# Moving a pool of SBUF tiles and a few queued steps in a chunk-attention and FFN kernel

## The chip, the cores and the metric

The kernel runs on one core of one Trainium2 chip. The metric is the device time of one execution in microseconds (us). The profile is of one such execution; its trace holds every instruction of the five engines: TensorE (PE, with its weight loads shown apart as PEld), VectorE (DVE), ScalarE (ACT), GpSimd (POOL) and SyncE (SP, which only issues DMAs here).

## The reference

Attention inside chunks of 64 positions, then a normalised two-layer FFN with a residual. B = 8, H = 8, S = 576, D = 64, so 4608 rows of 512; the hidden layer has 2048 columns. All data is fp32.

```python
scores = matmul(q_c, k_c^T) / sqrt(D)          # per (batch, head, chunk of 64)
attn = exp(scores - max); attn = attn / (sum(attn) + 1e-9)
x = matmul(attn, v_c)                           # regrouped to (B, S, H * D)
xn = (x - mean(x)) / sqrt(var(x) + 1e-6) * g_ln
out = x + maximum(xn @ w_ch1, 0) @ w_ch2        # 512 -> 2048 -> 512
```

## The kernel before, in words

**Rows.** The 4608 rows are 18 pairs of 256 rows; two pairs are a tile, so there are nine tiles of 512 rows. Tiles 0 to 2 go through the FFN one by one (`ffn`); tiles 3 to 8 go in three units of two tiles (`unit_ffn`). Attention for a pair (`attention`) is a generator; so are the FFN streams. Nothing is scheduled by a tool: `play` reads strings of letters and takes one step of the named stream for each letter, and `weave` takes steps of side streams at given points of a unit. Each engine runs its own instructions in the order in which they were issued, so the strings and the places of the calls decide what stands behind what.

**Precision.** A product is done as three TensorE passes on split operands: a rounded high part (`h`) and the rest, the low part (`l`): high by high, high by low, low by high. A hidden block is made ready in two steps: a cast, ACT's Relu into the high part (L540 in `ffn`, L799 in a unit), and a rest, DVE's difference (L541 and L804).

**Tiles 1 and 2.** `SECOND` is the order of the side steps during tile 1's FFN, `THIRD` the one during tile 2's. The number is that of a token of the FFN (`u` is a block of 12 matmuls, up or down; `1` is the cast and rest behind an up block) before which the letters' steps are taken. `A` and `B` are the attention of tile 2's two pairs, `C` and `G` those of tile 3's, `D` and `H` those of tile 4's. `S` is `prepare`, which writes combined and split weights to DRAM for the units: for each of eight pairs of hidden blocks, sums on POOL (L635, then L643 to L646), a cast on ACT (L654), a rest on POOL (L656) and DMAs. `P` and `Q` are `combine`, which makes the units' operands from the transposed rows. In `attention`, the transposes of the probabilities are four steps of four DVE instructions (L358) or TensorE transposes, `den` is the step with the sums (L365 to L367), then come the 64 small output matmuls (L387), the step that scales them to `x` (L421), statistics, and transposes of the normalised rows (L467 on DVE, or L459 on TensorE with ACT's copy L460).

**Units.** The up product of a unit is done by a scheme with seven block products (2, 1, 6, 5, 7, 3, 4) in place of eight, for each of four quarters `q` of the hidden blocks and each of two halves `e`. Each block product is 6 matmuls (L777) into one of four PSUM banks; ACT copies a bank to SBUF (`snap`, L783) or DVE adds one to a snap (`hu`, L786). After the four quarters come two down halves, `n` = 0 and 1, each over 16 hidden blocks `f` with 12 matmuls of 512 columns (L860). Blocks get their cast and rest (`split`, `rest`) three blocks ahead. Block number i of a unit's 32 lies in the pool `hp` (tiles `hh`, `hl`) where i % 5 is 0 or 1, and in tiles `hx` of the pool `raws` where it is 2, 3 or 4; `raws` also holds the snaps of the up product. TensorE loads these blocks as the stationary operand and streams the weights (`ring`). Attention for the pairs of the next unit is woven into the first two units; the third has no side work.

**SBUF.** Pools lie one behind the other in the order in which they are made. Adding up their tiles per partition, `raws` (12 KiB) is the last and lies at 209.6 to 221.6 KiB; `x` (`keep`, four tiles of 4 KiB) lies at 152.3 to 168.3 KiB; `xt` (the ring and the transposed rows) and `hp` lie between them, `hp` ending at 208.3 KiB.

Of the kernel before, what the change touches and what calls it, by code (L numbers as in the profile page):

```python
# [10 lines left out]
F32R = mybir.dt.float32r  # L11
# [6 lines left out]
P = 128  # L18
B, H, S, D = 8, 8, 576, 64
DM = H * D  # L20
# [5 lines left out]
HP = H // 2  # L26
NK = DM // P
NF = DFF // P
# [8 lines left out]
UNITS = (NTILE - LEAD) // 2  # L37

SECOND = {
    0: "ABS", 1: "AS", 2: "S", 3: "AAS", 4: "AS", 5: "AAS", 6: "S", 7: "AS", 8: "AAS", 9: "AAS", 10: "AAS", 11: "BAS",  # L40
    12: "BAC", 13: "BS", 14: "S", 15: "BBS", 16: "BS", 17: "BBS", 18: "S", 19: "BS", 20: "BBCS", 21: "BBS", 22: "BBDS",
    23: "BCS", 24: "BC", 25: "CS", 26: "S", 27: "CCS", 28: "CS", 29: "CCS", 30: "CDS", 31: "CDDS", 32: "DS",
}
THIRD = {
    0: "CS", 1: "CS", 2: "DDG", 3: "D", 4: "DD", 5: "D", 6: "DG", 7: "GGH", 8: "DG", 9: "D", 10: "GGP", 11: "HGP",
    12: "GGP", 13: "GHP", 14: "GGHP", 15: "GHP", 16: "GP", 17: "HHGP", 18: "HGG", 19: "HGP", 20: "HP", 21: "HP",
    22: "H", 24: "H", 25: "H", 26: "QQ", 27: "QR", 28: "Q", 29: "QXXN", 30: "QQR", 31: "Q",
}
ROOMS = {1: (3, 9), 2: (6,)}

# [47 lines left out]
def chunk_attention_ffn(ctx: ExitStack, tc: tile.TileContext, qkv, v01, g, w, out):  # L98
# [3 lines left out]
    const = ctx.enter_context(tc.tile_pool(name="const", bufs=1))  # L102
    load = ctx.enter_context(tc.tile_pool(name="load", bufs=1))
    work = ctx.enter_context(tc.tile_pool(name="work", bufs=2))
    keep = ctx.enter_context(tc.tile_pool(name="keep", bufs=4))
    xtp = ctx.enter_context(tc.tile_pool(name="xt", bufs=2))
    hp_ = ctx.enter_context(tc.tile_pool(name="hp", bufs=2))
    small = ctx.enter_context(tc.tile_pool(name="small", bufs=4))
    gap = ctx.enter_context(tc.tile_pool(name="gap", bufs=1))
    gap.tile([P, 16], F32, name="gap")  # L110
    raws = ctx.enter_context(tc.tile_pool(name="raws", bufs=1))
    ps_a = ctx.enter_context(tc.tile_pool(name="ps_a", bufs=1, space=PSUM))
    ps_h = ctx.enter_context(tc.tile_pool(name="ps_h", bufs=2, space=PSUM))
    ps_y = ctx.enter_context(tc.tile_pool(name="ps_y", bufs=4, space=PSUM))
# [513 lines left out]
    def prepare():  # L628
        late = []
        for p in range(NF // 2):  # L630
            fe, q, e = 2 * p, p // 2, p % 2
            both = [wp[fe], wp[fe + 1]]
            t_ = raws.tile([P, 2, 2, PAIR], F32, name="sums", tag="wf")
            for i in range(2):
                nc.gpsimd.tensor_tensor(  # L635
                    out=t_[:, i], in0=both[i][:, 0, :DM].rearrange("p (a n) -> p a n", a=2).bitcast(F32),
                    in1=both[i][:, 1, :DM].rearrange("p (a n) -> p a n", a=2).bitcast(F32), op=ALU.add,
                )
            for i in range(2):
                nc.sync.dma_start(w2d[fe + i], both[i][:, :, DM:].bitcast(F32))  # L640
            yield
            a11, a12, a21, a22 = t_[:, 0, 0], t_[:, 0, 1], t_[:, 1, 0], t_[:, 1, 1]
            nc.gpsimd.tensor_tensor(out=a22, in0=a21, in1=a22, op=ALU.add)  # L643
            nc.gpsimd.tensor_tensor(out=a21, in0=a11, in1=a21, op=ALU.subtract)
            nc.gpsimd.tensor_tensor(out=a11, in0=a22, in1=a11, op=ALU.subtract)
            nc.gpsimd.tensor_tensor(out=a12, in0=a12, in1=a11, op=ALU.subtract)  # L646
            for to, of in late:
                nc.sync.dma_start(to, of.bitcast(F32))
            nc.sync.dma_start(wa[q][:, e, 0], both[0][:, :, PAIR:DM].bitcast(F32))
            nc.sync.dma_start(wa[q][:, e, 1], both[0][:, :, :PAIR].bitcast(F32))  # L650
            nc.sync.dma_start(wa[q][:, 6, e], both[1][:, :, PAIR:DM].bitcast(F32))
            yield
            r = raws.tile([P, 2, 2, 2, PAIR], F32R, name="parts", tag="raw")
            nc.scalar.copy(r[:, 0], t_)  # L654
            yield
            nc.gpsimd.tensor_tensor(out=r[:, 1], in0=t_, in1=r[:, 0].bitcast(F32), op=ALU.subtract)  # L656
            late = [
                (wa[q][:, 2 + e, 0], r[:, :, 0, 0]), (wa[q][:, 4 + e, 1], r[:, :, 0, 1]),
                (wa[q][:, 4 + e, 0], r[:, :, 1, 0]), (wa[q][:, 2 + e, 1], r[:, :, 1, 1]),
            ]  # L660
            yield
        for to, of in late:
            nc.sync.dma_start(to, of.bitcast(F32))
        yield
# [93 lines left out]
    def unit_ffn(u):  # L758
# [29 lines left out]
        more = []  # L788
# [19 lines left out]
        for q in range(NF // 4):  # L808
            banks = [ps_y.tile([P, DM], F32, name="y") for _ in range(4)]
            c_, a_ = banks[0::2], banks[1::2]  # L810
            h = [hu[2 * q], hu[2 * q + 1]]
            s = [snaps[:3], snaps[3:]]

            def pair_of():
                w = ring.take()[:, : 2 * DM].rearrange("p (i h n) -> p i h n", i=2, h=2)
                return w[:, 0], w[:, 1]

            steps = []
            for e in range(2):
                steps += [  # L820
                    (c_, e, "2", None),
                    (a_, e, "1", lambda e: (copy(s[e][0], a_[e]), add(h[e][:, 0, 0], c_[e], s[e][0]))),
                ]
            for e in range(2):
                steps += [
                    (a_, e, "6", lambda e: copy(s[e][1], a_[e])),
                    (c_, e, "5", lambda e: copy(s[e][2], c_[e])),
                ]
            for e in range(2):
                steps += [  # L830
                    (a_, e, "7", lambda e: add(h[e][:, 1, 1], a_[e], s[e][2])),
                    (c_, e, "3", lambda e: add(h[e][:, 1, 0], c_[e], s[e][1])),
                ]
            for e in range(2):
                steps += [(a_, e, "4", lambda e: copy(h[e][:, 0, 1], a_[e]))]
            for i, (bank, e, name, then) in enumerate(steps):
                if i % 2 == 0:
                    w01 = pair_of()
                product(bank[e], w01[i % 2], name, name in "215")
                yield 6  # L840
                if i % 2:
                    ring.fetch()
                if then:
                    then(e)
                if q == NF // 4 - 1 and name in "34":
                    (split if name == "3" else rest)(e)

        for n, g in ((2, "raw"), (1, "wf")):
            x = raws.tile([P, n, 2, DM], F32R, name="hx", tag=g)
            more.extend(x[:, i] for i in range(n))  # L850
        ahead = 3
        split(2)
        stores = []
        for n in range(2):
            ys = [ps_y.tile([P, DM], F32, name="y") for _ in range(4 - 2 * n)]
# [7 lines left out]
                )  # L863

            pairs = [first + 2 * n, first + 2 * n + 1]
            ws = {}
            for f in range(NF):
                ws[f] = ring.take()[:, : 2 * DM].rearrange("p (h n) -> p h n", h=2)
                if f < NF - 2:
                    i = n * NF + f + ahead  # L870
                    for at, (m, j) in enumerate(
                        [(m, j) for j in range(4) for m in range(3)] if f == 0 else
                        [(m, j) for m in range(3) for j in range(4)]
                    ):
                        down(f, ws[f], j, m)
                        if at % 4 == 3:
                            yield 4
                            if at == 3 and n == f == 0:
                                rest(2)
                            if at == 3 and f > 0 and i - 1 < 2 * NF:  # L880
                                split(i - 1)
                            if at == 7 and f > 0 and i - 1 < 2 * NF:
                                rest(i - 1)
                    ring.fetch()
                    if f == 6:
                        for pair in pairs:
                            back[pair] = unspill(pair)
                    for to, of in stores:
                        nc.sync.dma_start(to, of)
                    stores.clear()  # L890
            for j in range(4):
                for f in range(NF - 2, NF):
                    for m in range(3):
                        down(f, ws[f], j, m)
                yield 6
                pair, jj = pairs[j // 2], j % 2
                x = back[pair][:, jj, :]
                nc.vector.tensor_tensor(out=x, in0=ys[j], in1=x, op=ALU.add)
                row = pair * PAIR + jj * P
                if tail and n == 1:  # L900
                    nc.sync.dma_start(out[row : row + P, :], x)
                else:
                    stores.append((out[row : row + P, :], x))
                if n == 0 and j < 3:
                    split(NF + j)
                    rest(NF + j)
            ring.fetch()
            ring.fetch()
        for to, of in stores:
# [113 lines left out]
```

## Time and profile before

| what | value |
|---|---|
| time, median of 3 runs | 853.22 us (852.88 to 853.78) |
| the profiled execution's time | 852.65 us |
| its span in the trace | 850.9 us |
| PE busy, PEld busy | 836.7 us (98%), 682.4 us |
| DVE, ACT, POOL busy | 563.1, 271.1, 150.7 us |
| TensorE clock granted, mean | 0.999 |
| tile 1, tile 2 FFN (about) | 123 to 222 us, 222 to 329 us |
| units: up product, then down halves | 329 to 411 to 505; 505 to 588 to 682; 682 to 758 to 851 us |

Times inside the trace are counted from the start of the span. Each row of a group gives its count, busy time and mean duration in ns, then the idle time of its engine just before it and what ended it. In rows in order of time, the first number is the start, the second how long the merged instructions took; consecutive matmuls overlap in these rows, so the rate of matmuls is read from starts, not from durations.

### The profile page before, as it was taken

To read this page: it belongs to the slowest core of one execution; us is meant where nothing else is said; L and a number is where in the kernel's file an instruction comes from. 1 tells how busy PE (TensorE), PEld (TensorE's weight loads), DVE (VectorE), ACT (ScalarE), POOL (GpSimd) and SP (SyncE) were. 2 spreads that over 40 slices of the span, in tenths; PEclk is the share of its full clock that TensorE was granted. 3 is DMA by queue.
4 is the path that set the end of the run, shared out by engine and by line. 5 is a ranking of instruction groups with operands and counts; after the bars stand their busy time and mean duration, and the time that the engine had idled before them with its cause. 6 is when DMAs were issued, how large, how long until landed. Compare 5 with 4: busy or idle time off the path is not lost.

```text
span 850.9 us, 14618 instructions
## 1 busy us (share of the span) xinstructions
PE 836.7 (98%) x5850; PEld 682.4 (80%) x5850; DVE 563.1 (66%) x957; ACT 271.1 (32%) x425; POOL 150.7 (18%) x138
## 2 busy tenths in 40 slices
PE   7999999999999999999999999999999999999998
PEld 4888888878787888888787888887878888888886
DVE  6999957777546926797999927879999421232321
ACT  5766432222312322222342402334223222232220
POOL 0110006585701223000130400001302200000000
PEclk9999999999999999999999999999999999999999
DMA  9996508977860137776686768867658776656572
GB/s 361 331 301 184 192 7 288 328 273 257 315 199 26 62 138 260 232 251 201 247 313 211 290 182 292 280 211 248 235 200 269 238 244 195 189 194 241 191 274 104
DMA packets 69043, 192.60 MB, mean 226 GB/s; under 512 B 6640, under 2 KB 20976, under 8 KB 67056
## 3 DMA queue, kind: packets, MB, share of 16 engines
q1 hardware_dynamic: 67680, 186.95, 63.9%
q0 software_dynamic: 1296, 4.72, 2.9%
q8 instruction: 46, 0.75, 0.3%
q14 instruction: 21, 0.17, 0.1%
HBM read 147.08 MB, written 39.85 MB: 220 GB/s over the span
## 4 chain that ended last, share of the span: by engine, by line
PE 78%; DVE 15%; issue 2%; POOL 2%; ACT 1%; DMA 1%; SPq 0%; POOLq 0%; ACTq 0%; DVEq 0%
PE y L777 24%; PE y L860 14%; PE h L527 14%; PE y L551 13%; PE h L860 8%; DVE pt_sb L358 4%; DVE rows L467 3%; PE s L298 2%; DVE hx L804 1%; DVE hl L804 1%; DVE den L365 1%; DVE xt L500 1%; PE s L387 1%; DMA k_t<-qkv 1%; PE h L387 1%
## 5 line engine op out<-in xcount | busy, mean ns | idle before, releaser
L777 PE MATMUL y<-xc,ring 128*128 128x512 f32 x1008 | 232.0, 390 | 0.0
L777 PEld LDWEIGHTS y<-xc,ring 128*128 128x128 f32 x1008 | 188.4, 188 | 39.5
L860 PE MATMUL y<-ring,hx 128*128 128x512 f32 x486 | 130.7, 396 | 0.0
L527 PE MATMUL h<-xth,wp 128*128 128x512 f32 (+1 forms) x432 | 129.9, 371 | 0.6 <-DVE x L421 0.5
L860 PEld LDWEIGHTS y<-ring,hx 128*128 128x128 f32 x486 | 91.1, 188 | 21.1
L786 DVE TENSOR_TENSOR hu<-y,snap 128x512 f32<-128x512 f32 x72 | 49.2, 690 | 83.5 <-ACT snap L783 43.3
L551 PE MATMUL y<-wp,hh 128*128 128x512 f32 x376 | 96.3, 394 | 0.0
L527 PEld LDWEIGHTS h<-xth,wp 128*128 128x128 f32 x432 | 78.3, 188 | 15.8 <-DVE hl L541 1.0
L783 ACT COPY snap<-y 128x512 f32<-128x512 f32 x72 | 42.2, 587 | 121.8 <-PE y L777 121.8
L551 PEld LDWEIGHTS y<-wp,hh 128*128 128x128 f32 x376 | 69.1, 188 | 14.0
L730 POOL TENSOR_TENSOR xc<-rows,xc 128x512 fp32r<-128x512 f32 x42 | 58.1, 1397 | 125.5 <-ACT xc L729 120.8
L358 DVE STREAM_TRANSPOSE pt_sb<-p_sb 32x256 f32<-32x256 f32 x176 | 76.7, 436 | 3.5 <-ACT p_sb L333 0.5
L527 PE MATMUL h<-xtl,wp 128*128 128x512 f32 (+1 forms) x216 | 78.3, 367 | 0.0
L541 DVE SCALAR_TENSOR_TENSOR hl<-h,hh 128x512 fp32r<-128x512 f32 (+1 forms) x53 | 32.9, 627 | 66.4 <-ACT hh L540 66.0
L860 PE MATMUL y<-ring,hh 128*128 128x512 f32 x252 | 70.5, 390 | 0.0
L467 DVE STREAM_TRANSPOSE rows<-xg 32x256 f32<-32x256 f32 x144 | 62.7, 435 | 5.4 <-ACT xg L449 3.2
L804 DVE SCALAR_TENSOR_TENSOR hx<-hu,hx 128x512 fp32r<-128x512 f32 x54 | 42.8, 798 | 30.7 <-PE y L860 12.6
L540 ACT ACTIVATE hh<-h 128x512 fp32r<-128x512 f32 (+1 forms) x53 | 28.5, 545 | 104.7 <-PE h L527 104.7
L860 PEld LDWEIGHTS y<-ring,hh 128*128 128x128 f32 x252 | 47.4, 188 | 10.2
L437 POOL TENSOR_TENSOR rstd<-vare,mhalf 128x2 f32<-128x2 f32 x12 | 10.6, 885 | 241.1 <-DVE vare L436 241.1
L551 PE MATMUL y<-wp,hl 128*128 128x512 f32 x188 | 51.8, 390 | 0.0
L860 PE MATMUL h<-ring,hx 128*128 128x512 f32 x162 | 50.8, 394 | 0.0
(130 smaller groups left out, 992.9 us busy)
## 6 DMA issues: line engine op xcount, KB each, us to landing
ring<-w2d SPq DMA_DIRECT2D x96, 512.0 KB, 4.1
ring<-wa SPq DMA_DIRECT2D x84, 512.0 KB, 4.3
raw<-w SPq DMA_DIRECT2D x15, 1024.0 KB, 7.8
out<-x SPq DMA_DIRECT2D x36, 256.0 KB, 4.5
q_t<-qkv SPq DMA_DIRECT2D x17, 512.0 KB, 5.6
k_t<-qkv SPq DMA_DIRECT2D x17, 512.0 KB, 6.5
v_t<-qkv SPq DMA_DIRECT2D x32, 256.0 KB, 6.0
w2d<-wp SPq DMA_DIRECT2D x16, 512.0 KB, 6.0
```

The lines of the kernel that those rows point to most:

```text
L358: nc.vector.transpose(out=pt_sb[quad(2 * h2 + j), :, c, quad(i)], in_=p_sb[quad(2 * c + i), :, h2, quad(j)])
L467: nc.vector.transpose(out=to[quad(j), :, quad(i)], in_=of[quad(i), :, quad(j)])
L527: nc.tensor.matmul(h, lhsT=(wh, wh, wl)[m][:, ks], rhs=(xth, xtl, xth)[m][:, k, :], start=i == 0, stop=i == len(terms) - 1,)
L540: nc.scalar.activation(hh, h, AF.Relu)
L541: nc.vector.scalar_tensor_tensor(out=hl, in0=h, scalar=0.0, in1=hh.bitcast(F32), op0=ALU.max, op1=ALU.subtract)
L551: nc.tensor.matmul(sums(pairs[j // 2])[j % 2], lhsT=(hh, hh, hl)[m], rhs=(wh, wl, wh)[m], start=f == 0 and m == 0, stop=f == NF - 1 and m ...
L730: nc.gpsimd.tensor_tensor(out=o[:, 1], in0=x, in1=o[:, 0].bitcast(F32), op=ALU.subtract)
L777: nc.tensor.matmul(bank, lhsT=w[:, (0, 0, 1)[m], ks], rhs=x[:, (0, 1, 0)[m], k, :], start=start and k == m == 0, stop=k == 1 and m == 2, s ...
L783: nc.scalar.copy(out, bank)
L786: nc.vector.tensor_tensor(out=out, in0=bank, in1=s, op=ALU.add)
L804: nc.vector.scalar_tensor_tensor(out=hl, in0=x, scalar=0.0, in1=hh.bitcast(F32), op0=ALU.max, op1=ALU.subtract)
L860: nc.tensor.matmul(ys[j], lhsT=(hh, hh, hl)[m], rhs=w[:, (0, 1, 0)[m]], start=f == 0 and m == 0, stop=f == NF - 1 and m == 2,)
```

## The change

Three things are changed. The pool `keep` is made after `raws` instead of before `xt`: so `x` moves to the last 16 KiB that are used, 205.6 to 221.6 KiB, and `xt`, `hp`, `small` and `raws` each move down by 16 KiB (`raws` to 193.6 to 205.6 KiB). In the last quarter of a unit's up product, the casts and rests of blocks 0, 1 and 2 are issued with block products 7, 3 and 4 instead of 3, 4 and after them, and in a down half's first block the order of the matmuls is changed so that the four that need the low part come last; the rests at the turn from n = 0 to n = 1 are issued one bank later. In the strings, `prepare` gets one more (empty) step per pair of blocks between its sums and its cast, for which 8 letters `S` are added, two in `SECOND` and six in `THIRD`; and steps of the streams `A`, `B`, `G`, `H` and `P` are moved by one to three tokens.

```diff
-    0: "ABS", 1: "AS", 2: "S", 3: "AAS", 4: "AS", 5: "AAS", 6: "S", ...
-    12: "BAC", 13: "BS", 14: "S", 15: "BBS", 16: "BS", 17: "BBS", 18: "S", 19: "BS", ...
-    23: "BCS", 24: "BC", ...
+    0: "ABS", 1: "AS", 2: "S", 3: "AAS", 4: "AS", 5: "AS", 6: "AS", ...
+    12: "BACS", 13: "BS", 14: "S", 15: "BBS", 16: "BS", 17: "BS", 18: "BS", 19: "BS", ...
+    23: "BCS", 24: "BCS", ...
...
-    0: "CS", 1: "CS", 2: "DDG", 3: "D", 4: "DD", 5: "D", 6: "DG", 7: "GGH", 8: "DG", 9: "D", 10: "GGP", 11: "HGP",
-    12: "GGP", 13: "GHP", 14: "GGHP", 15: "GHP", 16: "GP", 17: "HHGP", 18: "HGG", 19: "HGP", 20: "HP", 21: "HP",
-    22: "H", 24: "H", ...
+    0: "CS", 1: "CS", 2: "DDGS", 3: "DS", 4: "DDS", 5: "DS", 6: "DGS", 7: "GGHS", 8: "DG", 9: "D", 10: "GGP",
+    11: "HGGP", 12: "G", 13: "G", 14: "GGHP", 15: "GHP", 16: "GHP", 17: "GP", 18: "HHGP", 19: "HGP", 20: "HGP",
+    21: "HHP", 22: "HP", 24: "H", ...
...
     work = ctx.enter_context(tc.tile_pool(name="work", bufs=2))
-    keep = ctx.enter_context(tc.tile_pool(name="keep", bufs=4))
     xtp = ctx.enter_context(tc.tile_pool(name="xt", bufs=2))
...
     raws = ctx.enter_context(tc.tile_pool(name="raws", bufs=1))
+    keep = ctx.enter_context(tc.tile_pool(name="keep", bufs=4))
...
             yield
+            yield
             r = raws.tile([P, 2, 2, 2, PAIR], F32R, name="parts", tag="raw")
             nc.scalar.copy(r[:, 0], t_)
...
-                if q == NF // 4 - 1 and name in "34":
-                    (split if name == "3" else rest)(e)
-
-        for n, g in ((2, "raw"), (1, "wf")):
-            x = raws.tile([P, n, 2, DM], F32R, name="hx", tag=g)
-            more.extend(x[:, i] for i in range(n))
+                if q == NF // 4 - 1 and name in "73":
+                    (split if name == "7" else rest)(e)
+                if q == NF // 4 - 1 and name == "4":
+                    if e == 0:
+                        for n, g in ((2, "raw"), (1, "wf")):
+                            x = raws.tile([P, n, 2, DM], F32R, name="hx", tag=g)
+                            more.extend(x[:, i] for i in range(n))
+                    (rest if e else split)(2)
+
         ahead = 3
-        split(2)
...
+            early, late = ((2, 3, 0), 1) if n else ((0, 2, 1), 3)
+            firsts = [(m, j) for m in range(2) for j in early] + [(0, late), (1, late)] + [(2, j) for j in (*early, late)]
...
-                        [(m, j) for j in range(4) for m in range(3)] if f == 0 else
+                        firsts if f == 0 else
...
-                            if at == 3 and n == f == 0:
-                                rest(2)
+                            if at == 3 and n > f == 0:
+                                rest(NF + 2)
...
                 if n == 0 and j < 3:
                     split(NF + j)
-                    rest(NF + j)
+                if n == 0 and 0 < j < 3:
+                    rest(NF + j - 1)
```

More of the change, by code (lines that the diff above doesn't have):

```diff
@@ L39 @@
 SECOND = {
-    0: "ABS", 1: "AS", 2: "S", 3: "AAS", 4: "AS", 5: "AAS", 6: "S", 7: "AS", 8: "AAS", 9: "AAS", 10: "AAS", 11: "BAS",
-    12: "BAC", 13: "BS", 14: "S", 15: "BBS", 16: "BS", 17: "BBS", 18: "S", 19: "BS", 20: "BBCS", 21: "BBS", 22: "BBDS",
-    23: "BCS", 24: "BC", 25: "CS", 26: "S", 27: "CCS", 28: "CS", 29: "CCS", 30: "CDS", 31: "CDDS", 32: "DS",
+    0: "ABS", 1: "AS", 2: "S", 3: "AAS", 4: "AS", 5: "AS", 6: "AS", 7: "AS", 8: "AAS", 9: "AAS", 10: "AAS", 11: "BAS",
+    12: "BACS", 13: "BS", 14: "S", 15: "BBS", 16: "BS", 17: "BS", 18: "BS", 19: "BS", 20: "BBCS", 21: "BBS", 22: "BBDS",
+    23: "BCS", 24: "BCS", 25: "CS", 26: "S", 27: "CCS", 28: "CS", 29: "CCS", 30: "CDS", 31: "CDDS", 32: "DS",
 }
 THIRD = {
-    0: "CS", 1: "CS", 2: "DDG", 3: "D", 4: "DD", 5: "D", 6: "DG", 7: "GGH", 8: "DG", 9: "D", 10: "GGP", 11: "HGP",
-    12: "GGP", 13: "GHP", 14: "GGHP", 15: "GHP", 16: "GP", 17: "HHGP", 18: "HGG", 19: "HGP", 20: "HP", 21: "HP",
-    22: "H", 24: "H", 25: "H", 26: "QQ", 27: "QR", 28: "Q", 29: "QXXN", 30: "QQR", 31: "Q",
+    0: "CS", 1: "CS", 2: "DDGS", 3: "DS", 4: "DDS", 5: "DS", 6: "DGS", 7: "GGHS", 8: "DG", 9: "D", 10: "GGP",
+    11: "HGGP", 12: "G", 13: "G", 14: "GGHP", 15: "GHP", 16: "GHP", 17: "GP", 18: "HHGP", 19: "HGP", 20: "HGP",
+    21: "HHP", 22: "HP", 24: "H", 25: "H", 26: "QQ", 27: "QR", 28: "Q", 29: "QXXN", 30: "QQR", 31: "Q",
 }
```

## The prediction

> **What bounds the kernel now.** I read the page first, then the waits, then PE's and DVE's rows in order of time.
>
> ```profile
> span 850.9 us, 14618 instructions
> PE 836.7 (98%) x5850; PEld 682.4 (80%) x5850; DVE 563.1 (66%) x957; ACT 271.1 (32%) x425; POOL 150.7 (18%) x138
> PE y L860 <- DVE hl L804: 2.3, 4, 0.9
> ```
>
> PE is busy for 98% of the span, so a change can gain in two ways only: by closing PE's stops, or by letting its matmuls follow each other faster. The wait row says that in the units PE stopped four times for a rest (L804), 0.9 us at the longest.
>
> Matmuls overlap, so their pace has to be read from starts. The third unit has no side work:
>
> ```profile
> 764.00 8.53 PE L860 MATMUL y<-ring,hx 128*128 128x512 f32 x36
> 772.37 1.98 PE L860 MATMUL y<-ring,hh 128*128 128x512 f32 x8
> 777.82 8.53 PE L860 MATMUL y<-ring,hx 128*128 128x512 f32 x36
> 786.19 1.98 PE L860 MATMUL y<-ring,hh 128*128 128x512 f32 x8
> 791.63 6.44 PE L860 MATMUL y<-ring,hx 128*128 128x512 f32 x27
> L860 PE MATMUL y<-ring,hx 128*128 128x512 f32 x486 | 130.7, 396 | 0.0
> L860 PE MATMUL y<-ring,hh 128*128 128x512 f32 x252 | 70.5, 390 | 0.0
> L860 PE MATMUL h<-ring,hx 128*128 128x512 f32 x162 | 50.8, 394 | 0.0
> L860 PE MATMUL h<-ring,hh 128*128 128x512 f32 x84 | 25.9, 389 | 0.0
> ```
>
> 36 matmuls that load `hx` take 772.37 - 764.00 = 8.37 us, 232.5 ns each, twice alike; the 24 on `hh` and `hl` from 786.19 to 791.63 take 226.7 ns each. The mean durations (396 and 394 against 390 and 389) say the same. Shape, clock and streamed ring are the same; what differs is where the stationary operand lies: `hx` above 209.6 KiB, `hh` and `hl` below 208.3 KiB. That is 5.8 ns on 486 + 162 = 648 matmuls, 3.8 us in all.
>
> Now the turn from block products to down halves, in the first unit (the second has the same rows 176.8 us later), where attention for the next unit is woven in:
>
> ```profile
> 411.55 0.61 PE L860 MATMUL y<-ring,hh 128*128 128x512 f32 x2
> 413.07 0.50 PE L860 MATMUL y<-ring,hl 128*128 128x512 f32 x1 [0.90 <-DVE hl L804]
> 456.05 0.62 PE L860 MATMUL y<-ring,hh 128*128 128x512 f32 x2
> 456.84 0.51 PE L860 MATMUL y<-ring,hl 128*128 128x512 f32 x1 [0.16 <-DVE hl L804]
> 411.50:456.00 44.50, 43.60 (x364) 34.93 (x364) 42.10 (x78) 16.14 (x28) 10.76 (x8) 1.00 0.71 249
> 430.34 1.35 DVE L804 SCALAR_TENSOR_TENSOR hx<-hu,hx 128x512 fp32r<-128x512 f32 x1 [1.13 <-ACT hx L799]
> 454.53 1.21 DVE L365 TENSOR_REDUCE den<-p_sb 128x16 f32<-128x1024 f32 x1
> 456.15 0.63 DVE L804 SCALAR_TENSOR_TENSOR hl<-hu,hh 128x512 fp32r<-128x512 f32 x1
> ```
>
> The third matmul of the half needs block 0's low part and waits until 413.07. The row of the stretch 411.5 to 456 (columns: PE, PEld, DVE, ACT, POOL) is the more important one: DVE is busy for 42.10 of 44.50 us, with one idle time over 0.2 us, the 1.13 shown. Block 15's rest (456.15) stands behind `den` and ends just as PE wants it. In the first down half of units 1 and 2 DVE is as much the bound as PE; in the second halves (34 of 49.5 us busy) and the third unit it isn't.
>
> **The change part by part.** *Stops in tiles 1 and 2.*
>
> ```profile
> 177.68 1.05 ACT L654 CAST parts<-sums 128x1024 fp32r<-128x1024 f32 x1 [4.39 <-POOL sums L646]
> 183.59 1.22 DVE L365 TENSOR_REDUCE den<-p_sb 128x16 f32<-128x1024 f32 x1
> 185.40 0.33 PE L387 MATMUL h<-v_t,pt_sb 64*64 64x64 f32 x4
> 186.38 1.15 PE L387 MATMUL h<-v_t,pt_sb 64*64 64x64 f32 x60 [0.65 <-DVE hl L541]
> 187.46 2.12 PE L551 MATMUL y<-wp,hh 128*128 128x512 f32 x8
> 230.40 1.05 ACT L654 CAST parts<-sums 128x1024 fp32r<-128x1024 f32 x1 [2.74 <-POOL sums L646]
> 231.99 0.66 PE L459 MATMUL s<-ident,xg 128*128 128x128 f32 x4 [0.79 <-ACT rows L460]
> 263.06 5.40 DVE L358 STREAM_TRANSPOSE pt_sb<-p_sb 32x256 f32<-32x256 f32 x12
> 271.13 0.34 PE L387 MATMUL h<-v_t,pt_sb 64*64 64x64 f32 x6
> 271.72 1.14 PE L387 MATMUL h<-v_t,pt_sb 64*64 64x64 f32 x58 [0.26 <-DVE pt_sb L358]
> 272.80 2.11 PE L551 MATMUL y<-wp,hh 128*128 128x512 f32 x8
> 274.74 1.07 PE L551 MATMUL y<-wp,hl 128*128 128x512 f32 x4
> 276.34 0.50 PE L527 MATMUL h<-xth,wp 128*128 128x512 f32 x1 [0.53 <-DVE x L421]
> ACT parts L654 <- POOL sums L646: 14.7, 5, 4.4
> ```
>
> The idle times in brackets are 0.65 + 0.79 + 0.26 + 0.53 = 2.23 us; each stop also costs a restart. By starts: 64 output matmuls take 1.09 us where nothing holds them (58 of them run from 271.72 to 272.80), but last from 185.40 to 187.46, 0.97 lost; the stop before 231.99 is 0.79 and a restart of some 0.16, 0.95 lost; 271.13 to 272.80 loses 0.58; four matmuls from 274.74 last 1.60 in place of 0.91, 0.69 lost. Sum 3.2 us.
>
> The first: `B`'s `den` (steps of 1.22, 0.65 and 0.25 us) stands on DVE ahead of the rest that frees the PSUM bank; token 18 puts it behind. DVE was late there because ACT's L654 waited 4.39 us for POOL's sums (177.68) with the hidden block's cast queued behind it. The second stop is the same wait alone (230.40), with the copy that PE needs queued behind. The empty step gives the sums (2.54 + 3.2 us) three tokens of 2.72 us in place of two. Third and fourth: the output matmuls wait for the last four transposes, then `x` stands behind `den` and two of `P`'s differences. With the fourth transposes at token 11, `den` alone at 12 and `P`'s two at 14 and 15, the transposes end near 270.3 (263.06 plus 16 of 0.45), the rest behind them near 270.95, against 271.13 wanted: 0.2 us of slack, the thinnest place. `x` then ends near 274.4, against 275.6 wanted. What is late next: the last pair of `prepare` ends six tokens later, on POOL ahead of `D`'s root (0.7 us), whose reader on ACT has two tokens in hand; SP issues 13 of its DMAs inside tile 2's FFN (4 of them there before), the last over 90 us ahead of their readers. `H`'s two late steps share token 21 and keep their end at 25, and `A`'s moved `den` had no stop. Those I cost at nothing; uncovered, each costs about one stop like these, 0.6 to 1.0 us. Bounds for this part: 3.2 gained, or stops of the same size elsewhere, nothing. I take 3.2, since each stop's releaser is moved out of its way.
>
> *The pool.* With `raws` below 205.6 KiB no operand of PE lies above 208.3. If the place is the cause, PE gains 5.8 ns on each matmul that loads `hx`: 216 in unit 3 and 108 in the second halves of units 1 and 2 each, 432 in all, 2.5 us. The 216 of the two first halves are counted below, since DVE has a say there. Does `x` pay for lying on top? VectorE and ScalarE work on `hx` there today:
>
> ```profile
> L804 DVE SCALAR_TENSOR_TENSOR hx<-hu,hx x54: 628/692/1774, 416.5 to 828.0; 128x512 fp32r<-128x512 f32 x54
> L804 DVE SCALAR_TENSOR_TENSOR hl<-hu,hh x42: 627/691/1735, 412.3 to 833.4; 128x512 fp32r<-128x512 f32 x42
> ```
>
> Medians of 692 and 691 ns: nothing. Bounds: 0 (the place is not the cause) and 2.5; I take 2.5, since the pace steps with the tile's name alone.
>
> *Casts and rests at the turn.* PE's stop at 413.07 goes: rest 0 now stands directly behind the two adds of half 0's products 7 and 3, near 407.5, and the first low matmul comes ninth, 8 x 0.227 us in. What is queued behind: the two adds that free the third bank come later by rest 0's 0.69 us, to about 411.15; PE wants that bank with its second matmul, at 411.78, so 0.6 us of cover. For each of units 1 and 2 PE could win 413.07 - 411.78 - 0.23 = 1.06 and 0.11 of restart here, 0.4 to 0.6 at block 15, and 0.63 from 108 faster loads: 2.2 to 2.4 us. But DVE's row of work to 456.78 is the same length, and PE can't pass block 15's rest. DVE gains only what its instructions lose to each other's neighbours:
>
> ```profile
> 413.45 2.55 POOL L730 TENSOR_TENSOR xc<-rows,xc 128x512 fp32r<-128x512 f32 x2 [20.57 <-ACT xc L729]
> 414.87 1.68 DVE L804 SCALAR_TENSOR_TENSOR hl<-hu,hh 128x512 fp32r<-128x512 f32 x1
> 591.61 1.74 DVE L804 SCALAR_TENSOR_TENSOR hl<-hu,hh 128x512 fp32r<-128x512 f32 x1
> ```
>
> Rest 1 takes 1.68 and 1.74 us where the median is 0.69, and ends 0.55 us after POOL's two instructions do (416.00). Near 411.2 it meets no POOL work and saves 0.99 and 1.05. Rest 2, then near 415.4, would meet the end of POOL's second (some 0.15 us). So DVE's row ends about 0.85 us sooner in each unit, 1.7 in both, and PE stops for the balance of about 1.4 us: first at the second group of 64 output matmuls (today 0.27 us behind its transposes), then at block 15. Bounds: 0, and 2.25 + 2.4 = 4.6 if DVE didn't bind. I take 1.7, the value of the row that binds.
> [...]
>
> *The order in the first block and the later rests at n = 1* (first needed 1.8 us into that half) add no work; their cover is that 1.8 us, about a rest and two adds, and uncovered they'd cost a rest, 0.7 us.
>
> **Sum.** 3.2 + 2.5 + 1.7 = 7.4 us off the profiled execution's 852.65 us (span 850.9 and 1.75 around it), 845.25. The median of the runs shown, 853.22, is 0.57 above that execution, so I predict 845.8 us.
>
> **Rivals.**
> (a) DVE doesn't bind: PE takes the whole of its 4.6 us at the turns. 3.2 + 2.5 + 4.6 = 10.3, so 842.9. For it: much of DVE's row is issued ahead of need. Against it: the 42.10 of 44.50 us.
> (b) The pool's place does nothing, because what slows `hx` isn't its height (its base lies 128 bytes off a multiple of 256, `hh`'s doesn't, and the move by 16 KiB keeps that). Then 3.2 + 1.7 = 4.9 and 848.3.
> [...]
> (c) The stops in tiles 1 and 2 only move: a bank freed 0.2 us late, `prepare` beside `D` and `G`. Then 2.5 + 1.7 = 4.2 and 849.0.
> (d) Slower: ACT's cast L654 also waits for the DMAs that empty its tile:
>
> ```profile
> ACT parts L654 <- DMA wa<-parts: 9.2, 2, 5.3
> ```
>
> If the pairs now done in tile 2 held ACT like that twice with no cover, 9.2 us, less 7.4, makes 1.8 slower: 855.0. It decides from 7.4 us of exposed holds. Against it: today's two holds show in none of PE's stops, and the cast now comes a token later.
>
> **How the numbers follow.** Forecast 0.45, (a) 0.15, (b) 0.20, (c) 0.12, (b) and (c) together (1.7 gained, 851.5) 0.04, (d) 0.04. The forecast's own range, with 1 us on the turns and on the moved stops, is 844.6 to 847.2. The range 843.2 to 849.4 leaves out most of (a), (d), and the last of (c). 0.2% is 1.7 us, about what a measurement of this kernel tells from no change. Faster by more: all but (d) and (b) with (c), 0.92; within: the latter, 0.04; slower: (d), 0.04.
>
> **What would show it.** Pool: L860's rows for `hx` at 390 ns and a pace of 226.7 ns in the third unit; else (b). Turns: no stop at the third matmul of a half, rest 1 at 0.69 us, DVE still over 42 us busy in the stretch, PE stopping for L358 or for block 15's rest later on; with no such stop, (a). Tiles: the four stops gone and the ACT wait of 14.7 us near nothing. I'd be wrong if DVE's work were delayed at the turn (the third bank) or if a new ACT wait stood in tile 2.

## The result, and the profile after

The change makes the kernel faster: 848.95 us (median of 4 runs, 848.35 to 849.28) against 853.05 us (4 runs, 852.73 to 853.78) for the kernel before, a ratio of 0.995 with a 95% interval of 0.9933 to 0.9967. Predicted were 845.8 us and a range of 843.2 to 849.4. The time lies near the upper end of the range, 0.65 us from the 848.3 of rival (b): the move of the pool did nothing, as the rows below show.

The profiled execution took 849.28 us, 3.37 less than that of before. From the page:

```profile
L863 PE MATMUL y<-ring,hx 128*128 128x512 f32 x486 | 130.8, 396 | 0.0
L863 PE MATMUL y<-ring,hh 128*128 128x512 f32 x252 | 69.0, 390 | 0.0
```

From PE's waits (us in total, times, longest):

```profile
PE h L527 <- DMA wp<-wfs: 1.3, 1, 1.3
PE y L863 <- DVE hl L805: 0.7, 2, 0.4
PE y L778 <- DVE hu L787: 0.4, 2, 0.2
```

Two lines of the kernel before have new numbers here: L860 is L863 and L777 is L778. The matmuls that load `hx` still take 396 ns in the mean where those on `hh` take 390. The waits for a rest are down from 2.3 us in four to 0.7 in two; new are two short ones of L778 and one of 1.3 us for a DMA. PE in the third unit, in order of time:

```profile
760.61 8.53 PE L863 MATMUL y<-ring,hx 128*128 128x512 f32 x36
768.98 1.98 PE L863 MATMUL y<-ring,hh 128*128 128x512 f32 x8
```

36 matmuls in 768.98 - 760.61 = 8.37 us, as before: not a nanosecond of the pool's 2.5 us came. Tiles 1 and 2, PE in order of time:

```profile
186.62 1.16 PE L387 MATMUL h<-v_t,pt_sb 64*64 64x64 f32 x64
187.71 2.11 PE L551 MATMUL y<-wp,hh 128*128 128x512 f32 x8
231.28 0.60 PE L459 MATMUL s<-ident,xg 128*128 128x128 f32 x4
270.37 1.16 PE L387 MATMUL h<-v_t,pt_sb 64*64 64x64 f32 x64
274.32 0.39 PE L527 MATMUL h<-xth,wp 128*128 128x512 f32 x1
```

ACT's waits for the tile of the cast:

```profile
ACT parts L655 <- DMA wa<-parts: 8.7, 4, 3.9
ACT parts L655 <- POOL sums L646: 1.3, 1, 1.3
```

None of PE's rows has a bracket: all four stops are gone. The first 64 output matmuls now last 187.71 - 186.62 = 1.09 us, their undisturbed length. Comparing PE's starts one by one with those of before, the four places give 0.92, 1.00, 0.57 and 0.83 us, 3.3 together. ACT waits 1.3 us for POOL's sums, where it waited 14.7.

The turn in the first unit and block 15's low part later in the same half, on PE:

```profile
403.73 4.47 PE L778 MATMUL y<-xc,ring 128*128 128x512 f32 x19
408.39 1.66 PE L778 MATMUL y<-xc,ring 128*128 128x512 f32 x6 [0.19 <-DVE hu L787]
409.88 1.98 PE L863 MATMUL y<-ring,hh 128*128 128x512 f32 x8
411.70 1.07 PE L863 MATMUL y<-ring,hl 128*128 128x512 f32 x4
454.06 0.51 PE L863 MATMUL y<-ring,hl 128*128 128x512 f32 x1 [0.30 <-DVE hl L805]
```

On DVE:

```profile
405.24 0.68 DVE L805 SCALAR_TENSOR_TENSOR hl<-hu,hh 128x512 fp32r<-128x512 f32 x1
407.64 1.29 DVE L787 TENSOR_TENSOR hu<-y,snap 128x512 f32<-128x512 f32 x2
408.85 0.68 DVE L805 SCALAR_TENSOR_TENSOR hl<-hu,hh 128x512 fp32r<-128x512 f32 x1
413.19 1.18 DVE L805 SCALAR_TENSOR_TENSOR hx<-hu,hx 128x512 fp32r<-128x512 f32 x1
```

On POOL:

```profile
411.27 4.26 POOL L731 TENSOR_TENSOR xc<-rows,xc 128x512 fp32r<-128x512 f32 x3 [20.54 <-ACT xc L730]
```

And the busy times in that stretch (PE, PEld, DVE, ACT, POOL, then the granted clock, the DMA share and GB/s):

```profile
409.80:454.10 44.30, 44.00 (x368) 35.29 (x366) 41.82 (x79) 15.51 (x27) 10.82 (x8) 1.00 0.71 253
```

The half opens clean: eight matmuls on `hh` take 411.70 - 409.88 = 1.82 us, and the low part is there. Before, the stop at the third matmul cost 413.07 - 411.55 - 0.45 = 1.07 us and 0.11 of restart. But there is a new stop one step earlier, at the last block product: 408.39 - 403.73 is 4.66 us for 19 matmuls, 0.35 more than at 226.7 ns each, and the six behind it take 0.13 more than 6 x 226.7. Rest 1 (408.85) has its 0.68 us; rest 2 (413.19) takes 1.18 beside POOL. DVE's 41.82 of 44.30 us and block 15's stop (454.06) are still there. By PE's starts each of the two turns gives 0.62 us, counted to behind block 15.

That leaves the wait for `wp<-wfs`, an accumulating DMA from POOL's queue, at 54.56 us: PE lost 1.1 us there that it hadn't lost before, and 0.1 ahead of it. The sum by PE's starts is -3.3 (tiles) + 0 (pool) - 1.24 (turns) + 1.2 (start) = -3.3 us; the two profiled executions differ by 3.37.

### The profile page after: what moved, and what is told of

The parts are those of the page before. It is cut to its first block, busy times and chain, and to the rows that moved or that the text cites. A ratio compares the mean times of both kernels' runs of the same rounds, so it can differ in the third digit from the quotient of the medians.

```text
span 847.5 us, 14613 instructions
## 1 busy us (share of the span) xinstructions
PE 835.6 (99%) x5850; PEld 682.8 (81%) x5850; DVE 559.5 (66%) x957; ACT 271.1 (32%) x425; POOL 151.1 (18%) x138
## 4 chain that ended last, share of the span: by engine, by line
PE 80%; DVE 14%; DMA 2%; issue 2%; ACT 1%; POOL 0%; SPq 0%; ACTq 0%; DVEq 0%; POOLq 0%
PE y L778 24%; PE y L551 15%; PE h L527 14%; PE y L863 14%; PE h L863 8%; DVE pt_sb L358 3%; DVE rows L467 3%; PE s L298 2%; DVE hx L805 1%; DMA wp<-wfs 1%; PE h L387 1%; DVE top L305 1%; DMA k_t<-qkv 1%; DVE hu L787 1%; DVE hl L805 1%
## 5 line engine op out<-in xcount | busy, mean ns | idle before, releaser
L778 PE MATMUL y<-xc,ring 128*128 128x512 f32 x1008 | 232.6, 391 | 0.4 <-DVE hu L787 0.4
L778 PEld LDWEIGHTS y<-xc,ring 128*128 128x128 f32 x1008 | 188.4, 188 | 40.6 <-DVE hu L787 1.2
L863 PE MATMUL y<-ring,hx 128*128 128x512 f32 x486 | 130.8, 396 | 0.0
L863 PEld LDWEIGHTS y<-ring,hx 128*128 128x128 f32 x486 | 91.2, 189 | 21.1
L863 PE MATMUL y<-ring,hh 128*128 128x512 f32 x252 | 69.0, 390 | 0.0
L863 PEld LDWEIGHTS y<-ring,hh 128*128 128x128 f32 x252 | 47.4, 188 | 10.2
L863 PE MATMUL h<-ring,hx 128*128 128x512 f32 x162 | 50.8, 394 | 0.0
```

The source lines that it names most:

```text
L778: nc.tensor.matmul(bank, lhsT=w[:, (0, 0, 1)[m], ks], rhs=x[:, (0, 1, 0)[m], k, :], start=start and k == m == 0, stop=k == 1 and m == 2, s ...
L863: nc.tensor.matmul(ys[j], lhsT=(hh, hh, hl)[m], rhs=w[:, (0, 1, 0)[m]], start=f == 0 and m == 0, stop=f == NF - 1 and m == 2,)
```

## The experiments

E1 to E4 were timed together with the kernel before (853.13 us, 17 runs), then E5 to E8 (853.27 us, 17 runs), then E9 to E12 (852.99 us, 17 runs). E9 to E11 are single executions, read by their traces. In the expectations H is the theory that the height of `hx` makes it slow, O that its offset does, D that DVE binds in the first down halves.

| | edit | us, median (runs) | ratio to before, 95% |
|---|---|---|---|
| E1 | before + pool moved | 853.5 (12) | 1.0006 (0.9997 to 1.0015) |
| E2 | before + 128 bytes ahead of `raws` | 849.78 (5) | 0.9961 (0.9949 to 0.9973) |
| E3 | before + strings and empty step | 850.10 (5) | 0.9964 (0.9952 to 0.9976) |
| E4 | after + 128 bytes ahead of `raws` | 844.80 (6) | 0.9914 (0.9899 to 0.9929) |
| E5 | before + turn | 851.45 (12) | 0.998 (0.9972 to 0.9989) |
| E6 | E4 with the pool in its old place | 845.45 (4) | 0.9911 (0.9899 to 0.9924) |
| E7 | E4 + `combine` later | 845.36 (4) | 0.9909 (0.9896 to 0.9921) |
| E8 | E7 + rests 0 and 1 one product later | 843.80 (4) | 0.9895 (0.9881 to 0.9908) |
| E9 | after + 128 bytes ahead of `hp` | 853.91 (1) | |
| E10 | after, `raws` 64 bytes off | 849.6 (1) | |
| E11 | after, `raws` 192 bytes off | 847.83 (1) | |
| E12 | E8 with `combine` at 420 | 849.81 (12) | 0.9967 (0.9954 to 0.9979) |

**E1: the pool alone.**

```diff
-    keep = ctx.enter_context(tc.tile_pool(name="keep", bufs=4))
     xtp = ctx.enter_context(tc.tile_pool(name="xt", bufs=2))
...
     raws = ctx.enter_context(tc.tile_pool(name="raws", bufs=1))
+    keep = ctx.enter_context(tc.tile_pool(name="keep", bufs=4))
```

> The kernel before with the pool of x made last and nothing else. Theory O (offset: hx is slow because its base lies 128 bytes off a multiple of 256, which the move by 16 KiB keeps) and theory T (the cause is in the tile's use, not its address) both expect hx matmuls at 232 ns from start to start and 0 us gained from them. Theory H (height, the prediction's) expected 226.7 ns and 3.8 us, and has no support left in the changed kernel's trace. For the new stop of 1.3 us near 54 us in the changed kernel (PE waiting for an accumulating DMA into the weights): theory M (the move causes it) expects it here, 1.1 to 1.5 us slower than before; theory C (the landing time of that DMA is by chance) expects no such stop or one of another size, and a time within 0.5 us of before.

Measured: no gain (ratio 1.0006). `hx` now begins at 193.6 KiB, and is as slow as it was at 209.6; its third unit:

```profile
766.59 8.53 PE L860 MATMUL y<-ring,hx 128*128 128x512 f32 x36
774.95 1.98 PE L860 MATMUL y<-ring,hh 128*128 128x512 f32 x8
```

8.36 us for 36. The height is not the cause.

**E2: the offset alone.** The gap tile ahead of `raws` grows from 64 to 192 bytes; `raws` then begins on a multiple of 256 bytes, still above 209 KiB.

```diff
-    gap.tile([P, 16], F32, name="gap")
+    gap.tile([P, 48], F32, name="gap")
```

> The kernel before with the gap tile grown from 64 to 192 bytes: raws, and with it hx, starts 128 bytes further up, on a multiple of 256, and stays above 209 KiB. Theory O expects hx matmuls at 226.7 ns, 2.5 us gained in the third unit and the second down halves, and in the first down halves of units 1 and 2 a longer stop at block 15 in place of a gain: 850.5. Theories H and T expect 232 ns and no change, 853.0.

Measured: 0.9961 of before, 3.35 us. The third unit:

```profile
761.19 8.32 PE L860 MATMUL y<-ring,hx 128*128 128x512 f32 x36
769.35 1.98 PE L860 MATMUL y<-ring,hh 128*128 128x512 f32 x8
```

769.35 - 761.19 = 8.16 us for 36, 226.7 ns each, the pace of `hh`. So the offset costs 5.8 ns a matmul; on 648 matmuls that is 3.8 us. 128 bytes of padding, in a kernel otherwise as it was, gained four fifths of what the whole change gained. That is by medians (849.78, where 850.5 was expected); by PE's starts in the two profiled executions the units gain 2.9 us, and 1.3 more lie ahead of them, mostly in the start and at the first stop in tile 1, neither of which the edit was meant to touch. PE waited 2.6 us for rests (2.3 before): in the first down halves part of the faster pace is given back.

**E3: the strings and the empty step alone**; the strings are those of the change.

```diff
-SECOND = {...}, THIRD = {...}   # of before
+SECOND = {...}, THIRD = {...}   # of the change
...
             yield
+            yield
             r = raws.tile([P, 2, 2, 2, PAIR], F32R, name="parts", tag="raw")
```

> The kernel before with the strings and the empty step of prepare alone. If the four stops of tiles 1 and 2 carry this part: 3.2 us gained, 849.9, with all four gone and none new. If they only move: 852 to 853.

Measured: 850.10 us, 3.0 less than before. By PE's starts the four places give 0.92, 1.00, 0.57 and 0.83 us, the same numbers as in the whole change, and ACT waits 1.3 us for the sums. No stop of their size appeared elsewhere.

**E4: the change with the offset mended**, by the edit of E2.

> The changed kernel with the gap tile of 192 bytes, so hx at a multiple of 256 and below 206 KiB. Theory O: 226.7 ns, 2.5 us gained on the changed kernel, 846.4, and at block 15 of the first halves the stops grow by about 0.6 us each since DVE binds there. Theory T: 848.9, no change. If DVE does not bind in the first halves: 3.8 us gained, 845.2.

Measured: 844.80 us, 4.15 less than the changed kernel. Third unit:

```profile
757.18 8.32 PE L863 MATMUL y<-ring,hx 128*128 128x512 f32 x36
765.34 1.98 PE L863 MATMUL y<-ring,hh 128*128 128x512 f32 x8
```

PE's waits in the units:

```profile
PE y L863 <- DVE hl L805: 0.8, 2, 0.4
PE h L387 <- DVE pt_sb L358: 0.2, 1, 0.2
```

8.16 us again. Between this profiled execution and that of the changed kernel, PE's starts differ by 4.8 us: 1.9 ahead of the units, of which 1.6 are the start's wait for `wp<-wfs`, which isn't there, and 2.9 in the units, between the 2.5 and the 3.8 that the expectation gives with and without a bind. 648 x 5.8 ns would be 3.8: some 0.9 was given back at the first halves, at the second group of output matmuls (L387) and at block 15, where DVE binds. That is what the prediction said of the 108 faster loads in a first half.

**E5: the turn alone**, the whole part of the change's diff that lies in `unit_ffn`, of which these are the first lines.

```diff
-                if q == NF // 4 - 1 and name in "34":
-                    (split if name == "3" else rest)(e)
+                if q == NF // 4 - 1 and name in "73":
+                    (split if name == "7" else rest)(e)
...
```

> The kernel before with the casts, rests and first-block order of the units alone. Theory D (DVE binds the first down halves of units 1 and 2, so PE gets only what DVE's row is shortened by): the 1.06 us stop at the half's third matmul goes, a new one of about 0.35 us comes at the last block product, block 15's rest still stops PE, and 0.62 and 0.66 us are gained: 851.8. Theory F (PE is free to use what it wins): 2.2 us or more, 850.9 or less, with block 15's stop gone.

Measured: 851.45 us, 1.8 less than before (ratio 0.998): nearer D's 851.8 than the 850.9 or less without a bind; by PE's starts each turn gives 0.63. Its turns show the same rows as the changed kernel's: the stop at the last block product (0.4 us for two in the waits) and block 15's (0.7 for two). In its profiled execution the start's wait for `wp<-wfs` was 2.6 us; the pool isn't moved here, and in E4 it is moved and the wait is absent. So the move isn't what brings that wait; it comes with some executions.

Taken alone, the parts give -3.0 (E3), -1.8 (E5) and +0.4 (E1) by medians, -4.4 together, against -4.1 for the whole.

**E6: E4 with `keep` in its old place**, so that the offset is mended and the pool isn't moved.

```diff
+    keep = ctx.enter_context(tc.tile_pool(name="keep", bufs=4))
     xtp = ctx.enter_context(tc.tile_pool(name="xt", bufs=2))
...
-    gap.tile([P, 16], F32, name="gap")
+    gap.tile([P, 48], F32, name="gap")
     raws = ctx.enter_context(tc.tile_pool(name="raws", bufs=1))
-    keep = ctx.enter_context(tc.tile_pool(name="keep", bufs=4))
```

> The changed kernel with the pool of x back in its old place and the gap tile of 192 bytes. Theory O (offset alone): hx at 226.7 ns and the same time as with the pool moved and this gap, 844.8. If height or the pool's order has any part: slower than that by 0.5 us or more.

Measured: 0.9911 of before, E4 0.9914. By medians it is 0.65 us above E4, over the 0.5 that the expectation set as a sign of the pool. But the two profiled executions, 0.5 us apart, come apart between 53 and 58 us, in the start, and PE's starts keep that distance to within 0.1 us from there to the end: in the units the pool's place does nothing.

**E7: E4 with the first `combine` of a unit later**, to take DVE's load out of the first down half.

```diff
-FIRST_HALF = 345
+FIRST_HALF = 500
```

> The changed kernel with the gap of 192 bytes, and the eleven steps of the first combine of a unit begun at 500 in place of 345, so that its five differences on DVE and its work on POOL leave the first down half of units 1 and 2 for the second. Theory D: the stops at the second group of 64 output matmuls (0.32 and 0.42 us) and at block 15's rest (0.56 each, and restarts) go, some 2.0 us: 842.8; the two at the last block product (0.35 us each) stay. Theory F: those stops have another cause and stay, 844.8.

Measured: 845.36 us, no faster than E4. Both waits named in E4's last rows for L863 and L387 are gone, and PE's starts gain 1.12 and 1.23 us there: DVE did bind. But the second half gives 1.08 and 1.09 back. The stretch where the first new stop lies, columns as before, in E4:

```profile
461.00:471.00 10.00, 10.00 (x46) 8.29 (x45) 9.47 (x19) 5.45 (x10) 2.54 (x2) 1.00 0.84 305
```

In E7:

```profile
461.00:471.00 10.00, 9.91 (x43) 7.57 (x42) 9.76 (x17) 5.03 (x9) 5.34 (x4) 1.00 0.88 307
```

PE in E7, in order of time:

```profile
466.43 0.61 PE L863 MATMUL h<-ring,hx 128*128 128x512 f32 x2
467.13 0.73 PE L863 MATMUL y<-ring,hx 128*128 128x512 f32 x2
```

467.13 - 466.43 is 0.70 us for two matmuls, 0.25 lost, with no bracket: a stop under the view's limit, to be found by starts alone. The work that left the first half meets rests and transposes here: DVE 9.76 us of 10, POOL 5.34 where it had 2.54.

**E8: E7 with rest 0 behind half 1's product 3 and rest 1 behind half 0's product 4.**

```diff
-                if q == NF // 4 - 1 and name in "73":
-                    (split if name == "7" else rest)(e)
+                if q == NF // 4 - 1 and name == "7":
+                    split(e)
+                if q == NF // 4 - 1 and name == "3" and e:
+                    rest(0)
...
                 if q == NF // 4 - 1 and name == "4":
                     if e == 0:
+                        rest(1)
```

> As the run with the late combine, and rest 0 issued with half 1's block product 3, rest 1 with half 0's product 4, so that no rest stands on DVE ahead of the add that frees the bank of the last block product. If that order made the stops of 0.35 us: both go, 0.9 us with their restarts, 841.9. If not: 842.8.

Measured: 843.80 us. PE at the turn:

```profile
401.62 6.51 PE L778 MATMUL y<-xc,ring 128*128 128x512 f32 x28
407.97 1.98 PE L867 MATMUL y<-ring,hh 128*128 128x512 f32 x8
409.78 1.07 PE L867 MATMUL y<-ring,hl 128*128 128x512 f32 x4
```

28 matmuls in 6.35 us, 226.8 ns each: the stop at the last block product is gone, 0.49 and 0.48 us by PE's starts, and the low part is still in time. So it was rest 0, put ahead of the adds that free that product's bank (rest 1 stood behind them already). This is the fastest version: 9.5 us under before and 5.2 under the changed kernel (843.27 to 845.23).

**E9: the offsets exchanged.** 128 bytes ahead of `hp` in the changed kernel put `hh` and `hl` off a multiple of 256 and `hx` on one.

```diff
+    gap0 = ctx.enter_context(tc.tile_pool(name="gap0", bufs=1))
+    gap0.tile([P, 32], F32, name="gap0")
     hp_ = ctx.enter_context(tc.tile_pool(name="hp", bufs=2))
```

> The changed kernel with 128 bytes put ahead of hp: hp's tiles hh and hl now begin 128 bytes off a multiple of 256, and raws (hx) begins on one. Theory O (the offset of the stationary operand sets the pace): the signs change places. hx loads at 226.7 ns, hh and hl at 232.5; 36 matmuls on hx in the third unit take 8.16 us, 8 on hh 1.86. 648 hx matmuls give 3.8 us back, 378 + 126 on hh and hl in the units and 564 in the tiles cost 5.8 ns each, 6.2 us: some 2.4 us slower than the changed kernel, 851.3. Rival (something else of hx, its pool or its tile shape, is what was slow, and the gap in front of raws only happened to help): hh stays at 226.7, and the time is 845 to 849.

Third unit:

```profile
759.98 2.03 PE L865 MATMUL y<-ring,hh 128*128 128x512 f32 x8
761.85 1.08 PE L865 MATMUL y<-ring,hl 128*128 128x512 f32 x4
765.57 8.34 PE L865 MATMUL y<-ring,hx 128*128 128x512 f32 x36
773.74 2.03 PE L865 MATMUL y<-ring,hh 128*128 128x512 f32 x8
```

A stretch in the start:

```profile
57.00:60.30 3.30, 3.30 (x10) 2.56 (x9) 3.23 (x6) 2.61 (x5) 0.86 (x1) 0.52 0.73 272
```

The signs changed places: eight on `hh` take 1.87 us (234 ns each), 36 on `hx` 8.17 (227). The time is 4.6 us over the changed kernel's profiled execution in place of the expected 2.4. 2.0 of it lie in the start, where PE waited 2.04 us for `wp<-wfs` and the granted clock was 0.52 afterwards (last row). The other 2.6 are the offsets': by PE's starts the tiles lose 3.0 us (3.3 by the expectation's 564 matmuls) and the units gain 0.4 (0.8 by its counts).

**E10, E11: other offsets.** The gap tile left out (`raws` 64 bytes past a multiple of 256), and one of 32 elements (192 bytes past).

```diff
-    gap.tile([P, 16], F32, name="gap")
+    pass                                    # E10
+    gap.tile([P, 32], F32, name="gap")      # E11
```

> The changed kernel without the gap tile: raws begins 64 bytes past a multiple of 256. Theory O in its wide form (any base off a multiple of 256 is slow): 36 hx matmuls in the third unit take 8.37 us, the time is that of the changed kernel, 849. In its narrow form (only a tile whose rows begin in the second half of a 256-byte block): 8.16 us and some 845.

> The changed kernel with a gap of 128 bytes: raws begins 192 bytes past a multiple of 256. Wide form of O: 8.37 us for the 36 and 849, as at 64 and 128 bytes. Another dependence (on 64 or 128 bytes alone) would give 8.16 us at one of the offsets 64 and 192.

E10, then E11:

```profile
760.66 8.56 PE L863 MATMUL y<-ring,hx 128*128 128x512 f32 x36
769.06 2.01 PE L863 MATMUL y<-ring,hh 128*128 128x512 f32 x8
```

```profile
760.03 8.40 PE L863 MATMUL y<-ring,hx 128*128 128x512 f32 x36
768.27 1.98 PE L863 MATMUL y<-ring,hh 128*128 128x512 f32 x8
```

8.40 us at 64 bytes (233.3 ns each), 8.37 at 128 (232.5), 8.24 at 192 (228.9), 8.16 at 0 (226.7). Each offset costs, 192 the least; neither form of the expectation foresaw steps of different size.

**E12: E8 with `combine` begun at 420.**

```diff
-FIRST_HALF = 500
+FIRST_HALF = 420
```

> The version of e8 with the first combine stream begun at step 420 in place of 500, so that its work lies ahead of the stretch 461 to 481 us, where DVE was busy for 19.6 of 20 us and PE stopped twice for 0.25 to 0.29 us in each unit. Theory D (DVE's load in a stretch sets the stops): the stretch 451 to 461, where DVE had 2 us free, takes some of it; the two stops shrink or go, 842.0 to 843.5. Rival: the work now meets attention's in the first half and the stops at the second group of output matmuls and at block 15 come back, as with 345: 844.0 to 844.8.

Measured: 849.81 us, 6 us slower than E8: both expectations missed. PE at block 15 in both units:

```profile
451.77 0.63 PE L867 MATMUL y<-ring,hh 128*128 128x512 f32 x2
454.42 0.50 PE L867 MATMUL y<-ring,hl 128*128 128x512 f32 x1 [2.02 <-DVE hl L805]
628.63 0.62 PE L867 MATMUL y<-ring,hh 128*128 128x512 f32 x2
631.37 0.79 PE L867 MATMUL y<-ring,hl 128*128 128x512 f32 x1 [2.11 <-DVE hl L805]
```

DVE in the first:

```profile
450.83 0.68 DVE L734 TENSOR_TENSOR rows<-rows 128x512 f32<-128x512 f32 x1
451.43 1.20 DVE L365 TENSOR_REDUCE den<-p_sb 128x16 f32<-128x1024 f32 x1
452.67 0.87 DVE L366 TENSOR_SCALAR den<-den 128x16 f32<-128x16 f32 x1
453.74 0.63 DVE L805 SCALAR_TENSOR_TENSOR hl<-hu,hh 128x512 fp32r<-128x512 f32 x1
```

The stretches behind the two stops:

```profile
454.40:458.00 3.60, 3.58 (x16) 2.96 (x17) 3.04 (x6) 0.00 (x0) 0.00 (x0) 1.00 0.09 36
631.30:634.60 3.30, 3.23 (x8) 2.56 (x9) 1.90 (x4) 0.00 (x0) 0.00 (x0) 0.50 0.01 2
```

With 420, four of `combine`'s differences (L734) stand on DVE between 433 and 452 us, where E8 has none; the last comes right ahead of `den`, which takes 2.3 us, and block 15's rest stands behind both. It now starts at 453.74 where PE wanted its result near 452.2. The stops cost 2.20 and 2.29 us. The second was followed by 3.3 us at a granted clock of 0.50, some 1.6 us more; the first, 0.09 us shorter, by none. The twelve runs show how much of the 6 us is the clock: the two at a mean granted clock of 1.000 took 847.35 and 847.88 us, the four at 0.995 or 0.996 from 850.8 to 852.15.

## Why the prediction was right and wrong

**What bounds it: right.** PE's stops and its pace are what moved the time, and each gain in these runs is one or the other.

**Stops in tiles 1 and 2: right in place and size.** Predicted 3.2 us; the four places give 0.92, 1.00, 0.57 and 0.83, 3.3 in sum, where the prediction had 0.97, 0.95, 0.58 and 0.69. That the first came out so well is partly luck: with the strings of before, PE waited there 0.65 us in before, 1.2 in E1 and 0.2 in E2 and E5, and nothing here says why. What was costed at nothing cost nothing here: E3 alone is 3.0 us faster. Rival (c) falls. So does (d): ACT waited 8.7 us for DMAs in place of 9.2, and none of it reached PE.

**The pool: this step failed.** The prediction took the height of the operand for the cause "since the pace steps with the tile's name alone". That rows differ by name said only that something about `hx` is dear; two things differed, height and offset, and the offset was known and set down in rival (b). E1 and E2 part them: 8.36 us for 36 matmuls at a lower place, 8.16 at the old height with the offset mended; E9 turns the sign round. The term of 2.5 us is zero in this change. The size of the effect was right, 5.8 ns on 648 matmuls; the change does not touch it. The offsets run here cost from 2.2 ns a matmul (192 bytes in E11, 228.9 against 226.7) to 6.6 (64 bytes in E10, 233.3).

**The turn: right in mechanism, too large by 0.5 us.** Predicted 1.7, measured 1.24 by PE's starts (1.25 in E5's trace), 1.8 [0.9 to 2.4, from the interval of the ratio] in E5's median. Rest 1 took 0.68 as foreseen; rest 2, priced at 0.15 us for the end of POOL's second instruction, paid 0.50 (1.18 us, and 1.25 in the second unit), since POOL's row was 4.26 us with three instructions in it, 411.27 to 415.53; the two rests behind that row, at 417.87 and 419.01, take 0.63 and 0.68. And the third bank, at which the prediction saw 0.6 us of cover, had it; the bank that ran late was that of the last block product, of which the prediction said nothing. It is freed by the first of the same two adds, which ran in the kernel before at

```profile
409.19 1.29 DVE L786 TENSOR_TENSOR hu<-y,snap 128x512 f32<-128x512 f32 x2
```

The first of the two ended near 409.84, and PE wanted the bank six matmuls ahead of 411.55, at 410.19: 0.35 us of cover, less than rest 0's 0.69. E8 shows that rest 0's place made that stop. Of what it took, part would have gone to block 15 anyway: DVE binds there, as predicted (E7: 1.12 and 1.23 us gained with the load moved away). Rival (a) falls for the first half.

**The start was not in the sum.** The wait for `wp<-wfs` was absent in the profiled execution of before and 1.3 us in that of the changed kernel; it was 2.4 in E1 and 2.6 in E5, and absent in E4 and E8. It comes and goes with neither the pool's place nor the turn. What decides in one execution how late that DMA lands is open.

**By the sum.** 853.05 - 3.3 - 0 - 1.24 is 848.5; 848.95 was measured, with 848.35 to 849.28 in its runs. Of the 2.7 us between 848.5 and the predicted 845.8, the pool makes 2.5 and the turns 0.5; the tiles' 0.1 and the lower median of before (853.05 for 853.22) take 0.3 off. That the time lies in the predicted range is owed to its width, which takes in rival (b): the forecast's own range, 844.6 to 847.2, missed it, because it took the height of `hx` for the cause and left the offset to that rival, with a chance of 0.20.

## What to carry to other kernels

Where one operand is slower than another of the same shape, list everything in which they differ (height, offset, neighbours) and change one of them alone: a tile of padding answers in one run, and here it gained 3.4 us by itself. Moving an instruction to the front of a queue is priced at every reader of what it is put ahead of, also those that come before the place one is mending. Where an engine binds, moving its work is settled only by looking at each reader in the stretch it moves to: E8 and E12 differ in the start of one side stream alone, by 80 steps, and in time by 6 us.

## What the runs showed of the hardware that was not expected

TensorE's pace in a row of 512-column matmuls depends on where the stationary operand begins, in bytes past a multiple of 256: 226.7 ns at 0 (E2 and E4), 233.3 at 64 (E10), 232.5 at 128 (before and the changed kernel), 228.9 at 192 (E11), over 36 matmuls on `hx` each. At one offset the height made no difference (8.36 us for the 36 at 193.6 KiB in E1, 8.37 at 209.6 in before, both 128 bytes off). Only these four offsets were run. Why an offset costs time is open: the weight loads' own rows don't show it (188 ns in the mean for `hx` and for `hh` in before).

Behind some stops of 2 us and more TensorE's granted clock fell to about half for a stretch, behind others it did not. It fell behind those of 2.11 us in E12 (0.50 in the 3.3 us from 631.30), 2.04 in E9 (0.52 in the 3.3 us from 57.00) and 2.6 in E5 (0.72 in the mean from 50 to 54 us, 0.81 from 54 to 57, 1.00 from 57); it did not behind those of 2.02 in E12's first unit (1.00 from 454.40 to 458.00) and 2.4 in E1 (1.00 from 52 on, and in the mean of the execution), nor behind 1.3 in the changed kernel (1.00). So the length alone doesn't decide. Such a stop cost up to some 1.6 us more than its length here, an estimate from 3.3 us at 0.50.
